# A new hand-written order for three engines at the start of an attention and experts kernel

## The chip, the cores and the metric

The program runs on one core of one Trainium2 chip. The metric is device time in microseconds for one execution; lower is better. TensorE (PE) multiplies, VectorE (DVE) and ScalarE (ACT) do elementwise work, GpSimd (POOL) scatters and gathers rows, and the sync engine (SP) issues the plain DMAs.

## The reference

Inputs are q, k, v and a complex decay a_re + i a_im, each 4 x 8 x 768 x 48 (batch, head, position, channel), and the weights of a layer of eight experts. The recurrence and the layer behind it:

```
mag = sqrt(a_re^2 + a_im^2);  a = (a_re + i a_im) * min(mag, 0.999) / (mag + 1e-6)
for t in 0..767:                       # per batch and head, S is 48 x 48, complex
    S = diag(a[t]) S + k[t] v[t]^T
    y[t] = q[t] Re(S)
x = y of all heads, 3072 rows x 384
logits = x @ w_gate + softplus(x @ w_noise) * noise
top 2 of 8 experts, weights = softmax of the two logits
out = sum over the two of weight * (relu(x @ w1[e]) @ w2[e])
```

## The kernel before

**Tiles.** Positions are cut into six groups of 128, and a tile is one group of one batch: 24 tiles n = 4 g + b. The decays are handled in pairs of tiles, m = 0 to 11, because two tiles fit one instruction of 768 columns. The first two pairs (`HALVES`) are handled in halves a and b of 384 columns.

**One tile's work** has short names, and the whole start is written with them: a letter for the engine (A ScalarE, D VectorE, P TensorE, G the gate on all three), a number for the step, and the pair or the tile.

- Pair: A1 takes the logarithm of a_re, A2 its negative exponential, D1 the tangent of the angle, D2 its square, A3 log(1 + tan^2), D3 the log of the squared magnitude, A4 and D4 the clamp; A5 is the arctangent (D5 adds the angle carried from the group before).
- Tile: P1 sums the angles along positions, D6 (A6 from the second group on) and D7 reduce them to a fraction of a turn; D8 takes the absolute value, A7 and A8 are cosine and sine (both by `Sin`). P2 sums the log magnitudes, A9 and A10 are exp of plus and minus that, and D9 scales q and k by them. D10 and D11 rotate q and k; P3 and P4 transpose them, A11 and A12 evict the transposes (qT, kT).
- P5a, P5b are the scores (four heads each), D12a, D12b mask them, P6 and D13 update the state, D14 to D16 decay it, P7a, P7b give the output, A13 evicts it, P8 turns it back and A14 writes the rows. G0 to G12 compute the gate of a group and the slots of its rows; then POOL scatters the rows to the experts' lists.

**The order.** `ORDER` lists some 700 such names. For each of the three engines the names that belong to it are chained (`order at the start`), so the engine issues them in exactly that order; engines run in order, and an instruction waits at the head of its engine until its operands and buffers are free. The place of a name in the list also sets where its function emits its code, loads included (`PLACE`, `pos`, `behind_key`). Work that isn't in the list is placed by step numbers (`P`) and a scheduler.

**Table runs.** `Ln` and `Exp` need one activation table, `Arctan` and `Sin` another. `phase(i, ...)` puts an activation into run i; a table load opens each run, every activation of the run comes behind it, and the next load behind all of them. The run's number is a formula of the tile: even for logarithms and exponentials, odd for arctangents and sines.

**Buffers that matter.** EE (the exponentials A9 and A10) has three buffers, and each is also read by a small store to DRAM, `es<-ee`, which SP issues. `cum` has two PSUM banks, shared by P1, P2, P8 and the gate; `ptr`, the transposes, has one. SP issues in its own order: the first pairs' decays, q and k and v, the gate's weights, eight transfers `xs<-none` that mark rows as empty, and only then `es<-ee`.

**The experts** follow: for each, x @ w1 and h @ w2 in a split of two fp32r parts (L649, L698), nearly all on TensorE.

Of the kernel before, what the change touches and what calls it, by code (L numbers as in the profile page):

```python
# [77 lines left out]
def kernel(  # L78
# [103 lines left out]
    for t in ecol:  # L182
# [20 lines left out]
        A12.1 D10.3 P1.4 A13.0 D5.3 P3.2 A6.4 D16.0 D7.4 P5a.1 A11.2 D13.2 P1.5 D4.3 P4.2 D12a.1 A6.5 D4.2 P1.6  # L203
        A12.2 D7.5 P7a.1 D11.3 A6.6 P1.7 A8.2 D8.2 P6.3 A6.7 D7.6 A7.2 D7.7 P2.4 D13.3 A8.3 P8.0 D8.3 P5b.1
        A14.0 A7.3 P3.3 D12b.1 A9.4 P5a.2 P7b.1 D12a.2 P5b.2 A10.4 A13.1 D9.4 P2.5 A11.3 D12b.2 P7a.2 A1.4 D10.4
        P8.1 A9.5 P7b.2 D11.4 A2.4 P4.3 A10.5 D1.4 P6.4 A13.2 A14.1 D9.5 P8.2 A12.3 P2.6 D2.4 A14.2 P3.4 A9.6
        D11.5 A3.4 P5a.3 D10.5 A10.6 A11.4 P2.7 D9.6 P5b.3 A1.5 D12a.3 D10.6 P4.4 A9.7 A2.5 D12b.3 P7a.3 A12.4
        D3.4 P7b.3 A10.7 D1.5 P3.5 A13.3 A4.4 D9.7 G0.0 A11.5 D2.5 P5a.4 G1.0 D10.7 P4.5 A3.5 D12a.4 P5b.4 A12.5
        D3.5 P8.3 D12b.4 P3.6 A4.5 D4.4 P5a.5 A14.3 A5.4 D14.0 D16.1 D15.0 G2.0 P5b.5 G3.0 D15.3 G4.0 D15.1
        P7a.4 D12b.5 A5.5 D5.4 P7b.4 D5.5 P1.8 A11.6 D13.4 P1.9 A6.8 D12a.5 A13.4 D7.8 P6.5 A6.9 D4.5 P1.10 D7.9  # L210
        P7a.5 D11.6 A6.10 A8.4 D8.4 P1.11 D11.7 A7.4 P4.6 D15.2 A6.11 P7b.5 D7.10 A12.6 D7.11 P8.4 D8.5 A8.5
        P5a.6 D13.5 A7.5 P6.6 D12a.6 A14.4 G5.0 P3.7 P5b.6 A11.7 G6a.0 G6b.0 P2.8 G6c.0 D12b.6 G7.0 A13.5 P4.7
        G8a.0 G8b.0 A9.8 G8c.0 G8d.0 A10.8 P7a.6 G8e.0 A12.7 G8f.0 G8g.0 D9.8 P2.9 G9.0 G8h.0 P7b.6 D11.8 A9.9
        A1.6 D10.8 P2.10 A13.6 D13.6 A2.6 P5a.7 G12a.0 G12b.0 A9.10 G12c.0 P3.8 D1.6 A10.9 A10.10 G10.0 D12a.7
        A11.8 P8.6 G12d.0 G11a.0 G12e.0 G12f.0 P5b.7 G11b.0 A14.6 G12g.0 D9.9 P4.8 D12b.7 P2.11 D9.10 A12.8
        P7a.7 D2.6 A1.7 P6.7 D10.9 A9.11 A3.6 P7b.7 D10.10 A2.7 D3.6 P3.9 A13.7 A10.11 D1.7 P5a.8 A11.9 D11.9
        G0.1 A4.6 D12a.8 P5b.8 G1.1 D2.7 P4.9 D13.7 A3.7 P8.7 D12b.8 A12.9 P6.8 D3.7 P8.5 A14.7 D11.10 A4.7
        P3.10 D14.1 D16.2 D15.6 A14.5 P5a.9 D15.4 A5.6 D15.5 G2.1 P7a.8 G3.1 D12a.9 G4.1 P5b.9 D15.7 A5.7 D5.6
        P7b.8 D5.7 P1.12 A11.10 D12b.9 P1.13 D4.7 A6.12 A13.8 P4.10 D7.12 A6.13 D9.11 P1.14 A12.10 D7.13 P7a.9
        D10.11 A6.14 A8.6 P8.8 D7.14 P7b.9 D8.6 A14.8 D4.6 A7.6 P1.15 D13.8 A13.9 P5a.10 A6.15 D7.15 P6.9  # L220
        D12a.10 A8.7 P5b.10 D8.7 D13.9 A7.7 P2.12 D11.11 G5.1 P8.9 D12b.10 P7a.10 A14.9 P3.11 G6a.1 G6b.1 G7.1
        G6c.1 A9.12 G8a.1 P7b.10 G8b.1 A10.12 G8c.1 G8d.1 A11.11 D9.12 P2.13 A13.10 G8f.1 D10.12 P4.11 G9.1
        A9.13 A1.8 G8e.1 P8.10 G12a.1 G8g.1 A10.13 P6.10 G12b.1 G8h.1 G12c.1 A14.10 D9.13 A12.11 G10.1 G12d.1
        P2.14 G11a.1 G12e.1 A2.8 G12f.1 G11b.1 G12g.1 D10.13 P5a.11 A9.14 D11.12 A10.14 P3.12 D9.14 P5b.11
        A11.12 D12a.11 P2.15 D10.14 P7a.11 A1.9 D12b.11 A9.15 P4.12 D13.10 A2.9 D1.8 P7b.11 A12.12 D1.9 P6.11
        A13.11 D2.8 A10.15 P3.13 D11.13 A3.8 P5a.12 D2.9 A11.13 G0.2 D3.8 A3.9 P4.13 D12a.12 G1.2 A4.8 G2.2
        D13.11 P5b.12 G3.2 A12.13 D3.9 P6.12 G4.2 D12b.12 A4.9 P5a.13 D14.2 D11.14 A5.8 P3.14 D12a.13 P5b.13
        D15.8 D4.9 P7a.12 A5.9 D12b.13 P8.11 D5.8 P7b.12 A14.11 D16.3 D15.9 P1.16 D5.9 A11.14 P1.17 D13.12 A6.16
        D15.10 A13.12 P4.14 D7.16 A6.17 D9.15 P7a.13 A12.14 D7.17 P1.18 D10.15 A8.8 P7b.13 D8.8 A6.18 D4.8 A7.8
        P3.15 D7.18 A13.13 P1.19 D15.11 A11.15 P8.12 A6.19 P6.13 A14.12 D7.19 P5a.14 D8.9 A8.9 D11.15 P2.16 A7.9  # L230
        D12a.14 P5b.14 G5.2 D13.13 P7a.14 D12b.14 A9.16 G6a.2 P6.14 G6b.2 G7.2 G6c.2 A10.16 G8a.2 G8b.2 D9.16
        P4.15 G8c.2 P7b.14 D11.16 A12.15 G8d.2 P2.17 A13.14 D13.14 G8f.2 D10.16 P5a.15 G9.2 A1.10 G12a.2 P2.18
        G8e.2 A9.17 A2.10 D12a.15 P3.16 G8g.2 G12b.2 A9.18 G8h.2 G12c.2 D1.10 P7a.15 A10.17 A11.16 G12d.2 D2.10
        G10.2 A10.18 P5b.15 G11a.2 A3.10 G12e.2 G12f.2 G11b.2 G12g.2 P2.19 D9.17 P4.16 D12b.15 A9.19 A1.11 D3.10
        P7b.15 A12.16 D10.17 P8.14 A2.11 D9.18 P6.15 A14.14 P3.17 D1.11 A10.19 A4.10 D11.17 P5a.16 A13.15 D2.11
        P8.13 A11.17 G0.3 D10.18 A3.11 P4.17 D12a.16 G1.3 A14.13 P5b.16 D3.11 A12.17 D13.15 P8.15 A4.11 D14.3
# [836 lines left out]
```

## Time and profile before

| | |
|---|---|
| median of 3 runs | 709.5 us (709.18 to 710.33) |
| profiled execution | 710.01 us, span 708.3 us |
| busy, VectorE | 411.2 us (58% of the span) |
| busy, ScalarE | 328.0 us (46%) |
| busy, GpSimd | 172.6 us (24%) |
| TensorE's share of the chain that ended last | 80% |

The span runs from the first to the last instruction of the profile; the execution's own time is 1.7 us longer. A share of busy time is a mean over stages: the attention part, with all four engines at work, takes roughly the first 250 us, the experts the rest. "Granted clock" is the share of TensorE's full clock (2.4 GHz) that was granted in a stretch; 0.50 is the lower of its two levels, 1.2 GHz.

### The profile page before, as it was taken

To read this page: it belongs to the slowest core of one execution; us is meant where nothing else is said; L and a number is where in the kernel's file an instruction comes from. 1 tells how busy PE (TensorE), PEld (TensorE's weight loads), DVE (VectorE), ACT (ScalarE), POOL (GpSimd) and SP (SyncE) were. 2 spreads that over 40 slices of the span, in tenths; PEclk is the share of its full clock that TensorE was granted. 3 is DMA by queue.
4 is the path that set the end of the run, shared out by engine and by line. 5 is a ranking of instruction groups with operands and counts; after the bars stand their busy time and mean duration, and the time that the engine had idled before them with its cause. 6 is when DMAs were issued, how large, how long until landed. Compare 5 with 4: busy or idle time off the path is not lost.

```text
span 708.3 us, 13293 instructions
## 1 busy us (share of the span) xinstructions
PE 666.2 (94%) x5120; PEld 590.7 (83%) x5120; DVE 411.2 (58%) x919; ACT 328.0 (46%) x553; POOL 172.6 (24%) x183
## 2 busy tenths in 40 slices
...
GB/s 315 255 217 211 268 181 127 174 200 131 94 92 277 178 72 249 130 84 187 59 80 264 30 91 169 129 90 169 132 40 175 179 37 178 173 23 68 65 33 36
...
## 3 DMA queue, kind: packets, MB, share of 16 engines
...
q0 software_dynamic: 9360, 27.54, 11.0%
...
## 4 chain that ended last, share of the span: by engine, by line
PE 80%; DVE 8%; ACT 5%; DMA 4%; issue 1%; SPq 1%; another core or an unknown queue 0%; POOL 0%; POOLq 0%; DVEq 0%; ACTq 0%
PE po L698 28%; PE ph L649 27%; PE ptr L354 4%; PE psc L363 4%; PE pY L412 2%; PE cum L307 2%; DMA raw<-in_moe_w_dram 2%; PE pY L414 2%; PE px L625 2%; PE pG L374 2%; PE po L704 2%; PE cum L331 1%; PE psc L649 1%; ACT t L248 1%; PE cum L427 1%
## 5 line engine op out<-in xcount | busy, mean ns | idle before, releaser
L698 PE MATMUL po<-w2h,h 128*128 128x384 f32 x768 | 203.9, 338 | 2.1 <-DVE ao L709 2.1
L649 PE MATMUL ph<-x,w1h 128*128 128x512 f32 (+2 forms) x720 | 187.2, 348 | 0.6 <-ACT x L630 0.5
L698 PEld LDWEIGHTS po<-w2h,h 128*128 128x128 f32 x768 | 139.4, 188 | 3.7 <-DVE ao L709 3.6
L649 PEld LDWEIGHTS ph<-x,w1h 128*128 128x128 f32 x720 | 125.7, 189 | 18.3 <-DVE h L655 1.3
L698 PE MATMUL po<-w2l,h 128*128 128x384 f32 x384 | 128.5, 335 | 0.0
L649 PE MATMUL ph<-x,w1l 128*128 128x512 f32 (+2 forms) x360 | 124.4, 347 | 0.0
L710 POOL DMA_INDIRECT out_dram<-ao,ox x52 | 50.9, 978 | 261.2 <-DVE ao L709 247.2
L497 POOL DMA_INDIRECT xs<-xr,sl x48 | 60.8, 1266 | 202.4 <-DVE qk L336 92.0
L655 DVE SCALAR_TENSOR_TENSOR h<-ph,h 128x512 fp32r<-128x512 f32 (+2 forms) x144 | 69.6, 505 | 67.5 <-ACT h L651 51.0
L651 ACT ACTIVATE h<-ph 128x512 fp32r<-128x512 f32 (+2 forms) x120 | 59.9, 507 | 102.0 <-PE ph L649 73.3
L709 DVE SCALAR_TENSOR_TENSOR ao<-po,gw,ao 128x384 f32<-128x384 f32 (+1 forms) x52 | 31.8, 614 | 125.1 <-PE po L698 124.8
L630 ACT CAST x<-px 128x512 fp32r<-128x512 f32 (+1 forms) x42 | 21.3, 518 | 125.5 <-PE px L625 125.5
L649 PEld LDWEIGHTS ph<-x,w1l 128*128 128x128 f32 x360 | 67.9, 189 | 7.9
L698 PEld LDWEIGHTS po<-w2l,h 128*128 128x128 f32 x384 | 72.2, 188 | 0.1
L674 POOL DMA_INDIRECT ao<-out_dram,ox x49 | 54.7, 1117 | 53.7 <-issue 31.7
L363 PE MATMUL psc<-qT,kT 112*128 112x128 f32 x384 | 54.1, 283 | 1.1 <-DVE h L655 0.6
L363 PEld LDWEIGHTS psc<-qT,kT 112*128 112x128 f32 x384 | 48.9, 196 | 5.9 <-issue 1.9
L586 ACT CAST w2h<-raw 128x768 fp32r<-128x768 f32 x32 | 26.5, 835 | 33.6 <-PE po L698 17.3
L414 PE MATMUL pY<-am,v 128*48 128x128 f32 x384 | 38.3, 275 | 1.6 <-DVE am L364 1.6
L587 DVE TENSOR_TENSOR w2l<-raw,w2h 128x768 fp32r<-128x768 f32 x32 | 30.4, 957 | 15.1 <-ACT w2h L586 14.2
L364 DVE TENSOR_TENSOR am<-psc,mask 128x512 f32<-128x512 f32 x48 | 32.8, 684 | 10.2 <-PE psc L363 8.6
L412 PE MATMUL pY<-qT,z 112*48 112x128 f32 x320 | 34.2, 279 | 0.2 <-DVE z L397 0.2
...
## 6 DMA issues: line engine op xcount, KB each, us to landing
...
```

The lines of the kernel that those rows point to most:

```text
L363: key(f"P5{'ab'[half]}.{n}", nc.tensor.matmul(p[:, j, :], KT[n][:, h, :], QT[n][:, h, :], start=True, stop=True))
L364: LAST['am'] = nc.vector.tensor_mul(AM[n][:, 4 * half:4 * half + 4, :], p, mask[:, None, :].to_broadcast([128, 4, 128]))
L412: x = nc.tensor.matmul(o, Z[b][:, h, :], QT[n][:, h, :], start=True, stop=False, skip_group_check=True)
L414: x = nc.tensor.matmul(o, V[n][:, h, :], AM[n][:, h, :], start=not g, stop=True, skip_group_check=True)
L497: d = nc.gpsimd.indirect_dma_start(out=xs, out_offset=bass.IndirectOffsetOnAxis(ap=sl[:, kk, b:b + 1], axis=0), in_=XR[g][:, lo + b, :], i ...
L649: LAST['m'] = nc.tensor.matmul(p[:, :c], W1[e, kk][i][:, f * 128:(f + 1) * 128], XW[w, kk][:, j, 0:c], start=(m == 0), stop=(m == len(ms) ...
L651: nc.scalar.activation(h[:, 0:c], p[:, :c], AF.Relu)
L655: LAST['h'] = nc.vector.scalar_tensor_tensor(h[:, dst:dst + b - a], p[:, a:b], 0.0, h[:, a:b].bitcast(F32), op0=OP.max, op1=OP.subtract)
L674: nc.gpsimd.indirect_dma_start(out=ao[j][0:w, :], out_offset=None, in_=out, in_offset=bass.IndirectOffsetOnAxis(ap=OX[e][0:w, j:j + 1], ax ...
L698: LAST['po'] = key(f"PO.{e}.{j}", nc.tensor.matmul(p[:, :DM], HT[w, f][i][:, o:o + 128], W2[f // 2][k2][:, f % 2, :], start=(m == 0), stop ...
L709: nc.vector.scalar_tensor_tensor(a, p[0:n, :DM], g, a, op0=OP.mult, op1=OP.add)
L710: d = nc.gpsimd.indirect_dma_start(out=out, out_offset=bass.IndirectOffsetOnAxis(ap=OX[e][0:n, j:j + 1], axis=0), in_=a, in_offset=None, b ...
```

## The change

Four edits. `ORDER` is a new list, of 717 names instead of 710; it ends a little further on (P5a.17, P5b.17, P7a.17, A5.11, A13.16, D4.10, D5.10, D5.11 and D9.19 are in it, D10.18, D13.15, P3.18 and P6.16 no longer; D15.13 in place of D15.15). `phase` takes a name: the run's number is found by walking the list and raising it each time the kind of table changes; activations behind the list keep the formula, shifted by the difference at the list's end. The first pair's decays are loaded whole instead of in halves. The tiles of `softplus` have two buffers. The functions' other lines only pass the name.

```diff
     ORDER = """
-        A1a.0 A2a.0 D1a.0 A1b.0 D2a.0 A2b.0 A3a.0 D1b.0 D3a.0 D2b.0 A4a.0 A3b.0 D4a.0 A1a.1 D3b.0 P2.0 A2a.1
-        A1b.1 D1a.1 A4b.0 D2a.1 A2b.1 D4b.0 A3a.1 D1b.1 P2.1 A9.0 D3a.1 A10.0 D2b.1 A4a.1 D9.0 A3b.1 A9.1 D3b.1
-        A10.1 D4a.1 A4b.1 D9.1 A5a.0 D4b.1 A5b.1 P1.0 A5a.1 A5b.0 P1.1 D6.0 D7.0 P1.2 D6.1 D7.1 D8.0 A8.0 P1.3
-        D6.2 A7.0 D7.2 D6.3 P2.2 D10.0 D7.3 P3.0 D10.1 A8.1 P2.3 D8.1 A11.0 D11.0 A7.1 D11.1 P6.0 A1.2 P4.0
-        D13.0 P6.1 A9.2 D13.1 A2.2 A1.3 D1.2 A9.3 D2.2 A2.3 A12.0 D1.3 A3.2 P3.1 D2.3 A10.2 D3.2 A3.3 P5a.0 D9.2
-        A10.3 A11.1 D3.3 A4.2 P4.1 D10.2 A4.3 D11.2 P5b.0 A5.2 D12a.0 P6.2 D9.3 P7a.0 D12b.0 A5.3 D5.2 P7b.0
...
+        A1a.0 A1b.0 A2a.0 A2b.0 D1a.0 D1b.0 D2a.0 A1a.1 D2b.0 A3a.0 A2a.1 D3a.0 A1b.1 D1a.1 A4a.0 D2a.1 A2b.1
+        D4a.0 A5a.1 D1b.1 P2.0 D2b.1 A5a.0 A5b.1 P1.0 A5b.0 A9.0 D6.0 D7.0 A3b.1 A10.0 D3b.1 A3b.0 P1.1 D9.0
+        A4b.1 A3a.1 D3b.0 P1.2 D6.1 A4b.0 D3a.1 D7.1 A4a.1 D6.2 P1.3 A8.0 D8.0 D7.2 D6.3 D4a.1 A7.0 D7.3 D4b.0
+        A8.1 D8.1 P2.1 D11.0 A7.1 P2.2 D10.0 A9.1 P6.0 D4b.1 P3.0 D13.0 A10.1 A1.2 D9.1 P2.3 A11.0 D11.1 A1.3
+        P4.0 D10.1 A2.2 P6.1 A12.0 D1.2 A9.2 D13.1 P3.1 A2.3 D2.2 P5a.0 A10.2 D1.3 A9.3 A11.1 P5b.0 D12a.0 A3.2
+        D2.3 P4.1 A10.3 D12b.0 P7a.0 A3.3 D3.2 P7b.0 A12.1 D3.3 A4.2 P5a.1 D9.2 A4.3 P5b.1 D4.2 A13.0 D11.2 A5.2
+        P8.0 D10.2 P6.2 D12a.1 P3.2 A14.0 D5.2 A5.3 P7a.1 D13.2 P1.4 A11.2 D5.3 P1.5 A6.4 D9.3 P4.2 A6.5 D7.4
...
-    def phase(i, *args, **kw):
+    def usual(k):
+        a, i = k.split(".")
+        a, i = a.rstrip("ab"), int(i)
+        if a[0] == "G":
+            return 2 * min(i + 3, NG)
+        if a in ("A9", "A10"):
+            return 2 * (i // B) + 2 if i > 1 else 0
+        return 2 * (2 * i // B) + (a in ("A5", "A7", "A8"))
+    RUN, run, last = {}, 0, None
+    for k in ORDER:
+        if k.split(".")[0].rstrip("ab") in ("A1", "A2", "A3", "A4", "A5", "A7", "A8", "A9", "A10", "G5", "G7", "G9"):
+            run += (usual(k) - run) % 2
+            RUN[k], last = run, k
+    shift = run - usual(last)
+    def phase(name, *args, **kw):
+        i = RUN.get(name, usual(name) + shift)
         if i not in phases:
...
-        for j in range(2) if m == 0 else (slice(0, 2),):
-            nc.sync.dma_start(RE[m][:, j], a_in[m, 0][:, j])
-            nc.sync.dma_start(IM[m][:, j], a_in[m, 1][:, j])
+        nc.sync.dma_start(RE[m], a_in[m, 0])
+        nc.sync.dma_start(IM[m], a_in[m, 1])
...
-    c, w, u = (pool.tile(shape, F32, name=tag + x) for x in "cwu")
+    c, w, u = (pool.tile(shape, F32, name=tag + x, bufs=2) for x in "cwu")
```

Later in the new list, the names that the prediction speaks of stand so:

```
... P7b.1 A9.4 D12a.2 P5b.2 D13.3 P2.5 D12b.2 A13.1 A10.4 P7a.2 ...
... D3.4 A12.4 P7b.3 D10.6 A13.3 P3.5 ...
... G0.1 D15.4 A12.9 D11.10 P7a.8 G1.1 D4.7 A5.6 G2.1 ...
... G3.2 D15.11 A12.13 D5.8 P6.12 A13.12 G4.2 ... A6.17 G8e.1 P1.18 ... G12g.1 ...
... P2.12 D12b.10 G6a.1 P7b.9 A9.12 ... P2.13 G8b.1 A13.9 D13.9 D9.12 A11.11 P7a.10 ...
... G8g.2 G12b.2 G8h.2 G12c.2 D10.16 A9.17 G10.2 ...
```

## Rows read from the trace of the kernel before

**Rows 1.** the page, first part: busy us (share of the span), instructions

```profile
PE 666.2 (94%) x5120; PEld 590.7 (83%) x5120; DVE 411.2 (58%) x919; ACT 328.0 (46%) x553; POOL 172.6 (24%) x183
```

**Rows 2.** windows: us, busy us of each engine (instructions), TensorE clock, DMA share, GB/s

```profile
0.00:34.86 34.86, 13.52 (x96) 6.63 (x96) 24.79 (x61) 24.65 (x46) 5.41 (x27) 0.98 0.86 289
20.00:30.00 10.00, 7.13 (x88) 4.34 (x88) 8.42 (x14) 7.17 (x9) 0.00 (x0) 1.00 1.01 322
34.86:43.21 8.35, 8.20 (x80) 7.82 (x80) 8.31 (x13) 8.33 (x11) 0.00 (x0) 0.66 0.65 150
43.21:160.00 116.79, 116.17 (x1389) 94.53 (x1390) 107.96 (x222) 102.21 (x162) 24.73 (x18) 1.00 0.65 199
160.00:300.00 140.00, 130.86 (x1298) 111.73 (x1297) 105.47 (x339) 77.60 (x141) 39.81 (x40) 1.00 0.47 154
```

**Rows 3.** TensorE's waits: whole span, then 43-190 us (first, last of six)

```profile
PE ptr L354 <- ACT kT L355: 5.4, 1, 5.4
...
PE pY L414 <- DVE am L364: 0.8, 2, 0.5
...
PE cum L307 <- DVE t L302: 0.2, 1, 0.2
```

**Rows 4.** TensorE's timeline: start us, us, line, operation, tiles [idle before <-releaser]

```profile
34.86 1.96 PE L354 MATMUL ptr<-ident,qh 128*112 128x128 f32 x8 [5.38 <-ACT kT L355]
36.61 1.92 PE L363 MATMUL psc<-qT,kT 112*128 112x128 f32 x8
38.32 1.91 PE L354 MATMUL ptr<-ident,kh 128*112 128x128 f32 x8
40.03 1.30 PE L363 MATMUL psc<-qT,kT 112*128 112x128 f32 x8
41.26 0.93 PE L374 MATMUL pG<-v,kh 128*48 128x48 f32 x32
...
43.21 0.91 PE L307 MATMUL cum<-t,tri_t 128*128 128x384 f32 x2 [0.15 <-DVE t L302]
```

**Rows 5.** chain that ended last: start us, us to the next piece, what

```profile
52.81 0.88 PE ptr L354 x8
53.69 0.89 PE psc L363 x8
54.58 0.57 PE pY L414 x8
...
57.47 0.59 PE cum L427 x4
```

**Rows 6.** ScalarE's timeline

```profile
3.31 0.52 ACT L248 ACTIVATE t<-re 128x384 f32<-128x384 f32 x1 [1.20 <-DMA re<-in_a_dram]
...
5.53 0.52 ACT L248 ACTIVATE t<-re 128x384 f32<-128x384 f32 x1 [1.06 <-DMA re<-in_a_dram]
...
16.30 1.76 ACT L248 ACTIVATE t<-t 128x384 f32<-128x384 f32 x4
...
26.13 0.93 ACT L248 ACTIVATE tr<-tf,b_cos 128x768 f32<-128x768 f32 x1
27.07 1.28 ACT L247 ACT_TABLE_LOAD   x1
28.37 0.84 ACT L248 ACTIVATE t<-re 128x768 f32<-128x768 f32 x1
...
32.58 0.49 ACT L248 ACTIVATE ee<-cum 128x384 f32<-128x384 f32 x1 [1.44 <-DMA es<-ee]
```

**Rows 7.** SP's DMA issues

```profile
12.08 0.33 SPq L259 DMA_DIRECT2D im<-in_a_dram  x1
...
22.09 6.94 SPq L783 DMA_DIRECT2D xs<-none  x8
29.14 1.87 SPq L338 DMA_DIRECT2D es<-ee  x2
```

**Rows 8.** ScalarE by shape, 0-160 us: busy us, mean ns | idle before

```profile
L355 ACT ACTIVATE kT<-ptr 112x1024 f32<-112x1024 f32 x15 | 15.4, 1024 | 2.0 <-PE ptr L354 2.0
```

More of the change, by code (lines that the diff above doesn't have):

```diff
@@ L202 @@
-        A10.3 A11.1 D3.3 A4.2 P4.1 D10.2 A4.3 D11.2 P5b.0 A5.2 D12a.0 P6.2 D9.3 P7a.0 D12b.0 A5.3 D5.2 P7b.0
[L203 to L236, printed above, removed]
@@ new lines @@
+        P4.0 D10.1 A2.2 P6.1 A12.0 D1.2 A9.2 D13.1 P3.1 A2.3 D2.2 P5a.0 A10.2 D1.3 A9.3 A11.1 P5b.0 D12a.0 A3.2
+        D2.3 P4.1 A10.3 D12b.0 P7a.0 A3.3 D3.2 P7b.0 A12.1 D3.3 A4.2 P5a.1 D9.2 A4.3 P5b.1 D4.2 A13.0 D11.2 A5.2
+        P8.0 D10.2 P6.2 D12a.1 P3.2 A14.0 D5.2 A5.3 P7a.1 D13.2 P1.4 A11.2 D5.3 P1.5 A6.4 D9.3 P4.2 A6.5 D7.4
+        D7.5 P1.6 A12.2 D11.3 P1.7 A8.2 D10.3 P6.3 A6.6 D8.2 A6.7 D7.6 P3.3 A7.2 D7.7 D16.0 P2.4 D8.3 A8.3
+        D12b.1 P5a.2 A7.3 D4.3 P7b.1 A9.4 D12a.2 P5b.2 D13.3 P2.5 D12b.2 A13.1 A10.4 P7a.2 A11.3 D9.4 P8.1 P7b.2
@@ new lines @@
+        A9.5 D11.4 A14.1 P4.3 A10.5 D10.4 A13.2 P6.4 A1.4 D9.5 P8.2 A12.3 P2.6 D10.5 A2.4 P3.4 D11.5 A14.2 P5a.3
+        D1.4 A11.4 P5b.3 D2.4 A9.6 A10.6 P2.7 D12a.3 A3.4 D12b.3 P4.4 A9.7 D9.6 A1.5 P7a.3 D3.4 A12.4 P7b.3
+        D10.6 A13.3 P3.5 A2.5 D11.6 G0.0 A11.5 D1.5 P5a.4 A4.4 D2.5 P4.5 G1.0 A10.7 D4.4 P5b.4 A3.5 D12a.4 A12.5
+        G2.0 P8.3 D3.5 A14.3 P3.6 D12b.4 A4.5 G3.0 D14.0 P5a.5 G4.0 D15.0 A5.4 D4.5 P7a.4 D12a.5 P5b.5 D15.2
+        A5.5 D5.4 P7b.4 D5.5 P1.8 A11.6 D13.4 P1.9 D15.3 A6.8 D15.1 A13.4 P4.6 D7.8 A6.9 D12b.5 P1.10 A12.6 D7.9
@@ new lines @@
+        P7a.5 D9.7 A6.10 A8.4 D8.4 P1.11 D10.7 A7.4 P7b.5 D7.10 A6.11 D16.1 P3.7 A13.5 D7.11 D8.5 A8.5 P2.8 A7.5
+        P8.4 P5a.6 A14.4 G5.0 P6.5 D12a.6 P5b.6 D13.5 A9.8 G6a.0 A11.7 D11.7 P6.6 A10.8 D12b.6 P7a.6 G7.0 G6b.0
+        D9.8 P2.9 G6c.0 D10.8 P7b.6 A1.6 G8a.0 D11.8 A9.9 P4.7 A13.6 G8b.0 D13.6 A10.9 P2.10 G8c.0 A12.7 G8d.0
+        D9.9 P8.6 A9.10 P6.7 G8f.0 A14.6 D10.9 A10.10 P5a.7 G9.0 D11.9 A2.6 P3.8 D12a.7 P2.11 G8e.0 A11.8 D9.10
+        P5b.7 A9.11 D1.6 A1.7 P7a.7 D12b.7 A10.11 A2.7 P4.8 D2.6 P7b.7 D1.7 A12.8 P8.5 D10.10 A13.7 P3.9 A3.6
@@ new lines @@
+        D2.7 P5a.8 A14.5 A11.9 D3.6 P8.7 D13.7 P5b.8 A3.7 D12a.8 A14.7 P4.9 D3.7 A4.6 P6.8 D12b.8 A4.7 D14.1
+        D16.2 G0.1 D15.4 A12.9 D11.10 P7a.8 G1.1 D4.7 A5.6 G2.1 P7b.8 G3.1 D15.5 G4.1 D9.11 P3.10 A13.8 D5.6
+        P5a.9 A5.7 D13.8 A11.10 P8.8 D5.7 P1.12 A14.8 D10.11 P5b.9 A6.12 G12a.0 D7.12 P1.13 G12b.0 D12b.9 P4.10
+        A6.13 G12c.0 D12a.9 P1.14 D7.13 A12.10 G8g.0 D4.6 P7a.9 A6.14 G12d.0 A8.6 G8h.0 P1.15 D7.14 G12e.0 D8.6
+        G10.0 A6.15 D15.7 P3.11 A7.6 G11a.0 D7.15 G12f.0 G11b.0 P5a.10 A8.7 G12g.0 D8.7 D15.6 A7.7 P6.9 D12a.10
```

48 lines of the change are left out of this document (31 added, 17 removed).

## The prediction, made before the changed kernel was run

> **What bounds the kernel now.** I read four views, in this order. The page's first part: TensorE is busy for 666.2 us of the 708.3 us span [rows 1]. So there are 42 us without TensorE work, and a change that removes no matmul can win only from those, and from matmuls that run at the lower clock. Second, the windows show where they are: up to 34.86 us TensorE is busy for 13.5 us, that is 21.3 us idle; from 43.21 to 160 us it idles for 0.6 us, from 160 to 300 us for 9.1 us [rows 2]. Third, TensorE's waits: the one big entry that is not the first load is 5.4 us for ScalarE's kT, the eviction A12.0 [rows 3]. Fourth, the timelines of that place. TensorE starts P3.1 at 34.86 after 5.38 us of idling; the clock has fallen meanwhile, and P3.1, P5a.0, P4.1 and P5b.0 are followed by the next group after 1.75, 1.71, 1.71 and 1.23 us [rows 4], where such groups step 0.88 and 0.89 us later [rows 5]. A12.0 was late because ScalarE, in order, stood 1.44 us before A9.3 at 32.58, until the store es<-ee had landed, and because it had reached that run of its list only at 28.37, after the table load at 27.07 [rows 6].
>
> From 34.86 us on TensorE works nearly back to back. The sum is therefore a ledger of matmul work: how much more of it the new order has behind it at a given time.
>
> **The change, part by part.** (1) *Table loads.* In the old rule a run's number follows from the tile; in the new rule it rises whenever the order passes from an exponential or logarithm to an arctangent or sine, or back. Counted along both lists, the old one has loads 0 to 12, the new one 0 to 14: the start is cut into logs, four arctangents, logs, four sines. So two loads are added, both before 21 us. A switch is measured at 27.07: the sine before it ends at 26.13 + 0.93 = 27.06, the next activation starts at 28.37, so 1.31 us [rows 6]; two cost 2.6 us of ScalarE's time.
>
> The Trainium skill (ScalarE: Activation LUTs, What ACT_TABLE_LOAD costs) gives 1283 ns for the load and about 1380 ns more for a drain, 2.66 us for each switch to another set, and its rule is to batch activations by set. The trace has the first figure (1.28 us) and not the drain. By the Trainium skill's figure the two loads would cost 5.3 us instead of 2.6 us, and the lead worked out below would by an estimate be 1.6 us smaller, since 1.1 us of the 2.7 us would fall into a wait.
>
> (2) *The first load whole.* The first pair's logarithms were in halves before too; what changes is that both halves now come with one DMA of 384 KB. A1a.0 started at 3.31 with half the bytes, A1b.0 waited until 5.53 for its half [rows 6]. Both now start between these ends; I take 4.0. It decides nothing: the fifth activation, A1a.1, needs the second pair's data, the third 384 KB in the queue, which I put at 7.0 us; with 3.5 or 4.5 in place of 4.0 everything behind 7.1 us stays, and up to 1.1 us of lateness there falls into the wait for A9.3 (below).
>
> (3) *softplus with two buffers.* In the new list G8e.1 (which reads the tile) stands behind G4.2 (which writes it), so the second buffer lets the list be followed. It costs memory and no time.
>
> (4) *The order up to tile 16.* I laid the start out instruction by instruction: each engine in list order, each instruction when its operands, its PSUM bank and its engine are ready, durations from rows. The old list laid out in the same way gives A9.3 at 32.6, P3.1 at 34.9 and P1.4 at 43.3 us; the rows have 32.58, 34.86 and 43.21 [rows 4, 6]. The new list, by ScalarE:
> - Logs of run 0: A1a.0 4.0; A1a.1 7.1, A3a.0, A2a.1, A1b.1, A4a.0, A2b.1 at 0.41 to 0.53 us a step, end 9.9.
> - Load to 11.3. Four arctangents, 1.76 us for four [rows 6], end 13.0. Load to 14.3.
> - Run 2, eight half activations of which A4b.1, A4b.0 and A4a.1 each wait for a 0.55 us step of VectorE: end 19.0. Load to 20.3.
> - Four sines, 0.76 to 0.83 us a step (0.93 us for one [rows 6]), end 23.5. Load to 24.9. The old list was there at 28.37, so ScalarE leads by 3.5 us though it has loaded twice more.
> - A9.1, A10.1, A1.2, A11.0, A1.3, A2.2, A12.0 (29.0 to 30.0), A9.2, A2.3, A10.2, end 31.5. A12.0 now stands before A9.3, so P3.1 starts at 30.1, P5a.0 at 31.0, P5b.0 at 31.9.
> - A9.3 needs the first of three buffers, which es<-ee reads. That store stands in SP's queue behind the eight xs<-none transfers, issued from 22.09 to 29.03, and was issued at 29.14 [rows 7]; nothing in the change moves it ahead of them. So A9.3 again at 32.6, 1.1 us after ScalarE is ready. A11.1 (1.02 us for one eviction [rows 8]) ends at 34.0: P4.1 34.1, P7a.0 and P7b.0 until 36.1. A12.1 ends at 36.8: P5a.1 36.9, P5b.1 37.8. A4.3 ends at 38.3, load to 39.7, A13.0 until 40.3: P8.0 40.4, P6.2, P3.2, P7a.1 and then P1.4 at 43.1 us.
>
> P1.4 starts when it did (43.21), but five units more lie behind it: P5a.1 and P5b.1 (0.89 each), P3.2 (0.88), P7a.1 (0.57), P8.0 (at most 0.59, 0.5 taken) [rows 5]: 3.7 us, and 0.1 us for the earlier start: 3.8 us. Of that 2.8 us are the four groups that no longer run at the low clock (6.40 us from 34.86 to 41.26 [rows 4] against 3.54); the rest is idle time that is filled.
>
> What is late next: laid out further, the new list makes TensorE wait for A13.1 (P7a.2, 0.6 us), A12.4 (P3.5, 0.8), G1.1 (G2.1, 1.2), A13.9 (P7a.10, 0.4) and G8h.2 (G10.2, 0.6): 3.6 us up to 176 us. The old list's own waits from 43 to 190 us are six kinds, 0.8 us down to 0.2 us, together 2.5 us [rows 3]. That takes back 1.1 us. VectorE and ScalarE don't fall behind: at 176 us they lead by 4 and 3 us. The second gate's late half (G8e.1 to G12g.1) moves from 132 to 152 us, so POOL's scatters of that group come later; their reader, the buffer of tile 16's rows, isn't wanted before 185 us.
>
> (5) *Where the lead could grow.* SP waits before issuing the fourth pair's imaginary part until D1b.1 has ended, 12.08 us [rows 7]; in the new list D1b.1 ends at 10.7, so SP can be 1.4 us ahead with all that it issues behind. Whether es lands sooner depends on whether the transfers or SP set the pace up to 29 us: ends 0 and 1.1 us (then ScalarE is the bound), and 0.3 us taken, nearer to the transfers, since the 16 DMA engines are busy throughout from 20 to 30 us (share 1.01 [rows 2]).
>
> Sum: 3.8 - 1.1 + 0.3 = 3.0 us. After the list TensorE has 520 us of dense work whose amount is the same, so the lead should arrive at the end. The profiled execution took 710.01 us (span 708.3 and 1.7 around it), 0.5 us over the median: 707.0 us on that footing, 706.5 us as median.
>
> **Rivals.** *A: given back behind the list.* From 160 to 300 us TensorE idles for 9.1 us [rows 2], in stretches that no list governs, where gate, last tiles and first expert interleave. If work there falls differently, most of the 3.0 us can go. For it: these idles are three times the lead. Against: the lead is on all three engines, and the new list carries more of ScalarE's and VectorE's work (D4.10, D5.10, D5.11, D9.19, A13.16). 708.2 to 709.8 us.
>
> *B: more than the ledger.* es lands at 31.5 and the idles behind 160 us shrink because VectorE leads by 4 us and TensorE's waits there are partly for VectorE. 4 to 5.5 us: 704.0 to 705.5 us.
>
> *C: slower, by the clock.* The new start has matmuls in small groups: laid out, 10.6 us of work in the 16 us from 24.4 to 40.4. If the clock falls there and stays low, every us of dense work costs another (1.75 against 0.88 us for P3 [rows 4, 5]). The lead is gone once 3 us of matmul work more than laid out run at 1.2 GHz, and it is slower by over 1.4 us from 4.4 us on; with 7 us it is 4 us slower, 713.5 us. For it: the clock did fall in this stretch of the old order, to a mean of 0.66 between 34.86 and 43.21 [rows 2]. Against: that came after 5.4 us without a matmul; from 20 to 30 us, with 7.13 us busy of 10, the clock was granted in full [rows 2], and the new gaps from there on are 0.7 to 1.8 us.
>
> The Trainium skill (TensorE: Matmul & The Clock Gate, Part 1) says that half rate is the default and activity lifts it; the trace agrees so far as it fell behind the longest gap, 5.4 us.
>
> *D: it doesn't do what it says.* If es lands late (34 us) or the loads are placed ahead of evictions, the new front gains only 1.5 us: 708.0 us, inside A's and the forecast's bounds.
>
> **Chances.** The likeliest, the lead kept (2 to 4 us, 705.5 to 707.5 us), 0.60; A with D 0.20; B 0.10; C 0.10. A measurement can tell 0.2%, 1.4 us, from no change. Faster than 708.1 us: the forecast, B and a little of D, 0.71; within: 0.17; slower than 710.9 us: C and the worst of A, 0.12. The range that holds 8 in 10 runs from 704.3 us (half of B left out) to 709.8 us (all of A in, C out).
>
> **What would show it.** Fifteen table loads, two more before 21 us; the first sine near 20 us and the load behind the sines near 23.5 us. A9.3 again waiting for es<-ee, ending near 32 us. P3.1 near 30 us, no gap over 3 us between 24 and 43 us, and the granted clock at full after 22 us. P1.4 near 43 us with P5a.1, P5b.1, P8.0, P3.2 and P7a.1 before it. P7b.15 some 3 us earlier than before. I am wrong if A9.3 doesn't wait for the store, if the clock in 24 to 43 us is below full, or if the lead at 176 us is there and the end isn't earlier.

## The result: 1.3% slower, and the profile after

The changed kernel took 719.0 us (median of 4, 718.2 to 719.2) beside 709.4 us for the kernel before on the same chip: ratio 1.013 [1.011, 1.015], 9.6 us slower. The prediction said 706.5 us. The profiled execution took 718.8 us with a span of 717.0 us.

The page's first part after the change; against [rows 1] TensorE's busy time is 3.6 us more, and the span 8.7 us more:

```profile
PE 669.8 (93%) x5120; PEld 592.2 (83%) x5120; DVE 411.8 (57%) x919; ACT 331.2 (46%) x555; POOL 168.2 (23%) x183
```

The same windows of the changed kernel, to be laid beside [rows 2]:

```profile
0.00:34.86 34.86, 19.27 (x120) 11.31 (x120) 24.99 (x63) 28.27 (x50) 5.46 (x27) 1.00 0.84 290
20.00:30.00 10.00, 7.39 (x51) 4.71 (x51) 7.82 (x13) 7.97 (x11) 0.00 (x0) 1.00 1.02 321
34.86:43.21 8.35, 7.25 (x93) 5.96 (x92) 8.35 (x12) 8.32 (x12) 0.00 (x0) 1.00 0.88 193
43.21:160.00 116.79, 112.31 (x1356) 91.16 (x1355) 109.43 (x225) 101.88 (x160) 12.72 (x12) 1.00 0.61 181
160.00:300.00 140.00, 124.67 (x1257) 106.53 (x1256) 101.03 (x329) 74.29 (x136) 46.28 (x46) 0.98 0.49 159
```

Up to 43 us the change does what was forecast. Before 34.86 us 24 matmuls more have run (120 against 96 [rows 2]): P3.1, P5a.0 and P5b.0, 2.7 us of work by the steps of [rows 5]. TensorE is busy 5.75 us longer there; the other 3.1 us are a lower clock up to 28 us (see the steps that held). From 34.86 to 43.21 us the clock is at full where it had been 0.66. From 43.21 to 160 us TensorE idles for 4.5 us instead of 0.6 us, and from 160 to 300 us for 15.3 us instead of 9.1 us. TensorE's timeline of the front:

```profile
32.01 1.09 PE L367 MATMUL ptr<-ident,qh 128*112 128x128 f32 x8 [0.47 <-ACT kT L368]
32.94 1.95 PE L376 MATMUL psc<-qT,kT 112*128 112x128 f32 x16
34.98 1.06 PE L367 MATMUL ptr<-ident,kh 128*112 128x128 f32 x8
...
37.65 2.05 PE L376 MATMUL psc<-qT,kT 112*128 112x128 f32 x16 [0.60 <-ACT kT L368]
...
43.24 1.24 PE L321 MATMUL cum<-t,tri_t 128*128 128x384 f32 x3
```

P1.4 (43.24) starts where it did, with P5a.1 and P5b.1 (37.65) done, as laid out; the idle of 5.38 us before P3.1 [rows 4] is 0.47 us. So the lead was there, and it was lost later. The largest loss, in the timeline of all engines:

```profile
158.38 0.99 POOL L510 DMA_INDIRECT xs<-xr,sl  x1 [16.64 <-DVE am L377]
...
164.28 0.17 PE L490 MATMUL cum<-ohs,ones_b 128*128 128x8 bf16 x1
...
164.86 0.17 PE L490 MATMUL cum<-ohs,ones_b 128*128 128x8 bf16 x1 [0.41 <-issue]
165.57 0.18 PE L492 MATMUL cum<-ohs,tri_b 128*128 128x8 bf16 x1 [0.54 <-issue]
...
166.99 0.19 PE L490 MATMUL cum<-ohs,ones_b 128*128 128x8 bf16 x2 [1.24 <-issue]
167.61 0.98 POOL L510 DMA_INDIRECT xs<-xr,sl  x1 [0.30 <-issue]
...
169.84 0.27 PE L490 MATMUL cum<-ohs,ones_b 128*128 128x8 bf16 x4 [1.21 <-issue]
169.90 0.85 ACT L264 ACTIVATE t<-re 128x768 f32<-128x768 f32 x1 [6.37 <-PE cum L492]
...
170.23 0.19 DVE L494 TENSOR_TENSOR pos<-cum,base_run 128x32 f32<-128x32 f32 x1 [5.05 <-PE cum L490]
```

G10.2, fourteen matmuls of 8 columns of which only the first has to wait for an operand, is spread over 5.7 us: TensorE starts an instruction every 0.7 us or so, and "issue" says that it waits for no semaphore that the profile shows. ScalarE (6.37 us) and VectorE (5.05 us) wait behind it. All of this stands beside POOL's scatters, eight in one train from 158.38 to 168.6 us. In the kernel before, the same eight stand in two trains of four, from 137.1 and from 152.7 us, because the gate's late half was done by 132 us.

The hole has a second part. Behind it the granted clock falls to 0.50, the lower level, for 6.8 us:

```profile
168.03:174.85 6.82, 5.22 (x52) 4.38 (x52) 3.94 (x12) 4.25 (x8) 3.10 (x5) 0.50 0.51 173
```

TensorE is busy for 5.22 us of this at half speed, so about 2.6 us of the loss is the clock's (an estimate; eight transposes take 1.94 us at 169.96 and 1.04 us at 175.17 us).

### The profile page after: what moved, and what is told of

It is laid out like the page before. It is cut to its first block, busy times and chain, and to the rows that moved or that the text cites. A ratio compares the mean times of both kernels' runs of the same rounds, so it can differ in the third digit from the quotient of the medians.

```text
span 717.0 us, 13304 instructions
## 1 busy us (share of the span) xinstructions
PE 669.8 (93%) x5120; PEld 592.2 (83%) x5120; DVE 411.8 (57%) x919; ACT 331.2 (46%) x555; POOL 168.2 (23%) x183
## 3 DMA queue, kind: packets, MB, share of 16 engines
q0 software_dynamic: 9360, 27.54, 11.0%
## 4 chain that ended last, share of the span: by engine, by line
PE 77%; DVE 10%; ACT 5%; DMA 4%; issue 3%; another core or an unknown queue 0%; SPq 0%; POOL 0%; POOLq 0%; DVEq 0%; ACTq 0%
PE po L711 28%; PE ph L662 27%; PE ptr L367 4%; PE psc L376 3%; PE pY L425 2%; PE px L638 2%; PE pY L427 2%; PE pG L387 1%; DMA v<-in_v_dram 1%; PE cum L321 1%; PE psc L662 1%; PE po L717 1%; DVE qk L349 1%; DVE kh L357 1%; DVE am L377 1%
## 5 line engine op out<-in xcount | busy, mean ns | idle before, releaser
L510 POOL DMA_INDIRECT xs<-xr,sl x48 | 55.6, 1158 | 212.1 <-DVE z L410 113.4
L376 PE MATMUL psc<-qT,kT 112*128 112x128 f32 x384 | 51.7, 279 | 0.9 <-ACT kT L368 0.9
L376 PEld LDWEIGHTS psc<-qT,kT 112*128 112x128 f32 x384 | 47.0, 191 | 5.3 <-issue 1.9
L377 DVE TENSOR_TENSOR am<-psc,mask 128x512 f32<-128x512 f32 x48 | 32.5, 684 | 11.4 <-PE psc L376 8.2
```

The source lines that it names most:

```text
L376: key(f"P5{'ab'[half]}.{n}", nc.tensor.matmul(p[:, j, :], KT[n][:, h, :], QT[n][:, h, :], start=True, stop=True))
L377: LAST['am'] = nc.vector.tensor_mul(AM[n][:, 4 * half:4 * half + 4, :], p, mask[:, None, :].to_broadcast([128, 4, 128]))
L510: d = nc.gpsimd.indirect_dma_start(out=xs, out_offset=bass.IndirectOffsetOnAxis(ap=sl[:, kk, b:b + 1], axis=0), in_=XR[g][:, lo + b, :], i ...
```

## The experiments

Eighteen runs, of fourteen kernels, were made on five chips. The chips fall into two kinds by what the kernel before takes on them: 709.1, 708.5 and 709.6 us on three of them (as in the result above), 703.4 and 703.1 us on two. This difference turned out to be part of the answer. Times are medians; the ratio is to the kernel before on the same chip.

### First chip: the kernel before takes 703.4 us

The four expectations here were written for a chip of 709 us, so their ranges can be neither met nor missed; what counts is the difference to the kernel before.

**e1_gates_early.** In the new list, G8e to G12g of groups 0 and 1 moved back to where they stood relative to the other work.

```diff
-... G8d.1 P7b.10 ... A6.17 G8e.1 P1.18 ... G12g.1 D11.15 ...
+... G8d.1 G8e.1 P7b.10 ... P8.10 G12a.1 G8g.1 ... G11b.1 G12g.1 A9.14 ...
```

> The changed kernel with the late halves of the first two gates (G8e to G12g of groups 0 and 1) put back to where they stood relative to the other work in the old list; everything else as changed, so the two waits on PACE spread the scatters again. Theory T (the loss comes from POOL's scatters standing back to back in trains of 6 and 8, during which TensorE and ScalarE get their instructions late): trains of 2 to 4 as before, no 6 us hole at 163 to 170 us, 706 to 709 us, so 10 to 13 us under the changed kernel. Rival O (the new list's own waits and its instruction mix from 97 to 170 us lose the lead, the trains only coincide): 715 to 719 us. Rival F (a rest of 3 us lost in the trains of group 2 and later, which this doesn't move): 709 to 712 us.

700.9 us, 0.9973 [0.9949, 0.9996].

**e2_pace_only.** The new list untouched; the scatters of groups 0 to 2 wait for later tiles.

```diff
-(0, 1): 8, (0, 2): 9, (0, 3): 10, (1, 1): 11, (1, 2): 12, (1, 3): 13, (2, 1): 15, (2, 2): 15, (2, 3): 16,
+(0, 1): 9, (0, 2): 10, (0, 3): 11, (1, 1): 14, (1, 2): 14, (1, 3): 15, (2, 1): 16, (2, 2): 16, (2, 3): 17,
```

> The changed kernel, list untouched; only the tiles whose xT the scatters of groups 0 to 2 wait for are raised, so that from 155 us on the scatters come as 2, 4, 4, 4, 2 and not as 8, 2, 4, 2. Theory T: the hole at 163 to 170 us goes or shrinks to under 2 us, and the time falls by 4 to 8 us, to 711 to 715 us; what stays is what trains of 4 cost. Rival O: G10.2 and A1.10 stand where they stood, the hole stays, 717 to 720 us. If the late scatters hold up the first expert's rows instead, the time stays too, but with a wait on xg after 195 us.

702.4 us, 0.9981 [0.9962, 1.0000].

**e3_old_with_train.** The kernel before, with the eight scatters of group 1 in one train.

```diff
-(1, 1): 11, (1, 2): 12, (1, 3): 13,
+(1, 0): 13, (1, 1): 13, (1, 2): 13, (1, 3): 13,
```

> The kernel before, with one line changed: all eight scatters of group 1 wait for tile 13's xT, so they come back to back near 157 us as in the changed kernel; list, loads and buffers as before. Theory T: TensorE's instructions are issued 0.5 to 1.3 us apart near the end of the train, a hole of 4 to 7 us, 713 to 717 us. Rival O: no hole, 709 to 711 us, since the old list is the one that runs.

702.6 us, 0.9987 [0.9969, 1.0005]: no price, though the train is there. My theory of that hour (trains cost, everywhere) missed.

**e5_old_list.** The changed code with the old list.

> The changed code (free table runs, first load whole, softplus with two buffers) with the old list in place of the new one: 13 table loads again. Theory T and rival O alike put the whole loss into the list: 708.5 to 710.5 us. If the whole first load or the second softplus buffer had a price of their own, 711 us or more.

702.8 us, 0.9997 [0.9980, 1.0013]. Free table runs, the whole first load and the second softplus buffer have no price of their own.

### Second chip: 709.1 us

> The changed kernel itself, unaltered, as a control. The first four experiments ran on a chip where the kernel before takes 703.4 us and where no engine of any kernel shows a gap that ends in issue or remote between 43 and 260 us, the old list with all eight scatters in one train included; in the traces from which the prediction was judged, the kernel before took 709.4 us and has such gaps at the ends of trains. Theory T (scatter trains alone): 710 us or more here too, with the hole at 163 to 170 us. Theory T2 (a train stalls the engines only on a chip or in a condition in which it also delays them in the kernel before, by some us): where the kernel before runs at 703 us, this one runs at 700 to 702 us, with the 3 us of the forecast and no hole; where it runs at 709 us, 717 to 720 us. Rival O (the list's own waits): 9 us above the kernel before on any chip.

c1_after is the changed kernel itself: 718.6 us, 1.0144 [1.0124, 1.0165].

> Again the changed kernel with the late halves of the first two gates put back early, now beside the changed kernel on one chip. Theory T2: on a chip where the kernel before takes 703 us, within 1 us of the changed kernel; where it takes 709 us, 8 to 12 us under the changed kernel. Theory T: 8 to 12 us under it on any chip. Rival O: within 3 us of the changed kernel on any chip.

c2 is e1 again: 713.0 us, 1.0064 [1.0044, 1.0084], 5.6 us under the changed kernel beside it. That was less than the 8 to 12 us expected, and it is still 3.9 us over the kernel before, though its trains are of two and four again.

> Again the kernel before with the eight scatters of group 1 in one train behind tile 13. Theory T2: no price where the kernel before takes 703 us (702 to 704 us), 4 to 7 us where it takes 709 us, with TensorE's instructions issued far apart at the end of the train. Rival O: no price on any chip.

c3 is e3 again: 718.0 us, 1.0125 [1.0108, 1.0142], 8.9 us more where 4 to 7 us were expected. One line of PACE makes the old list as slow as the new one, here and not there. Twelve microseconds from the first scatter of the train; the columns are those of [rows 2]. First on the chip of 703.4 us, then on this one:

```profile
156.65:168.65 12.00, 11.79 (x161) 9.70 (x159) 10.80 (x36) 9.74 (x20) 8.72 (x8) 1.00 0.65 205
```

```profile
158.64:170.64 12.00, 5.20 (x69) 4.33 (x68) 3.66 (x6) 4.71 (x8) 8.05 (x8) 0.78 0.55 186
```

The program is the same, POOL does the same eight instructions, and in the second the other engines do less than half as much. In the timeline VectorE and ScalarE stand idle, and "remote" says that this view names nobody who holds them:

```profile
164.47 0.96 DVE L344 TENSOR_TENSOR kh<-qk,tr 128x768 f32<-128x768 f32 x1 [3.93 <-remote]
...
168.75 0.69 DVE L364 TENSOR_TENSOR am<-psc,mask 128x512 f32<-128x512 f32 x1 [3.33 <-remote]
...
169.46 0.49 ACT L248 ACTIVATE ee<-cum 128x384 f32<-128x384 f32 x1 [6.33 <-remote]
...
169.50 0.67 PE L414 MATMUL pY<-am,v 128*48 128x128 f32 x4 [6.80 <-DVE am L364]
```

The trace's semaphore records name it. The first three wait for the semaphore that only TensorE's instructions raise, and they start 0.02 to 0.03 us behind its records at 164.44, 168.73 and 169.44 us. The matmuls that raise it have their recorded (modelled) ends at 159.72, 160.81 and 161.45 us, so TensorE's signals came 4.7 to 8.0 us behind them; in e3 they come 0.01 to 0.03 us behind. So here too it is TensorE that holds the others, by late signals and not by late starts in its records.

### Third chip: 708.5 us

**x_full, x_thin, x_drop.** The old list, and eight scatters more in one train, into a tensor that nobody reads; in x_thin rows of 16 elements, in x_drop a bound of 0. So that the group's own scatters are done before, two entries of its pace are moved too, and six of these now stand in one train (136.8 to 147.8 us in x_full).

```diff
+xe = nc.dram_tensor("xe", [E * N, ROW], F32, kind="Internal").ap()      # x_thin: [E * N, 16]
...
-(1, 2): 12, (1, 3): 13,
+(1, 2): 'A12.13', (1, 3): 12,
...
+d = nc.gpsimd.indirect_dma_start(out=xe, out_offset=..., in_=none, in_offset=None,
+                                 bounds_check=E * N - 1, oob_is_err=False)   # x_drop: bounds_check=0
+behind.append((d, 13))
```

> The old list with all its own scatters in time (those of group 1 before 155 us), and eight more scatters of a constant tile, 128 rows of 1600 bytes each, into a tensor that nobody reads, in one train behind tile 13's xT. Theory T2 and all its forms: on a chip where the kernel before takes 709 us 6 to 10 us more, with VectorE, ScalarE and TensorE each starting instructions late between 160 and 171 us; where it takes 703 us, within 1 us. Rival: the hole came from the late rows of group 1 themselves (somebody waits for them), then no price here.

720.4 us, 1.0160 [1.0128, 1.0193], 11.9 us more, over the range. The train of six has a part in it: laid against the kernel before, the eviction A13.n of x_full ends 2.0 us later behind that train and 10.0 us later behind the train of eight.

> As x_full, but the eight added scatters write rows of 64 bytes instead of 1600. Form B of the theory (the bytes, that is the packets on the DMA engines, hold up the others): the price falls to under 2 us. Form N (the number of scatter instructions or of their rows and descriptors): the price stays, 6 to 10 us on a chip where the kernel before takes 709 us.

720.2 us, 1.0161 [1.0144, 1.0178], 11.7 us more.

> As x_full, but the bound of the added scatters is 0, so that practically every row is dropped and nothing is written. Form B: no price. Form N with the written rows as the cause: no price. Form P (POOL's own work on the descriptors, or what it does while it prepares them, is what holds up the others): the price stays, 6 to 10 us on a chip where the kernel before takes 709 us.

719.9 us, 1.0157 [1.0141, 1.0174], 11.4 us more. Nobody waits for these rows, and it doesn't matter how many bytes are written. In the twelve microseconds from the train's start, x_full moves 185 GB/s, x_thin and x_drop 51, and TensorE works 7.08, 7.06 and 6.74 us:

```profile
161.91:173.91 12.00, 7.08 (x84) 4.64 (x82) 6.10 (x23) 3.50 (x7) 8.49 (x8) 0.92 0.55 185
```

```profile
161.91:173.91 12.00, 7.06 (x84) 4.73 (x82) 6.17 (x23) 3.57 (x7) 8.43 (x8) 0.94 0.17 51
```

```profile
162.25:174.25 12.00, 6.74 (x91) 5.16 (x87) 5.86 (x14) 4.77 (x9) 8.29 (x8) 0.85 0.20 51
```

So it is not the bytes. Packets are there in all three: POOL's queue has 9872 of them in x_full and in x_drop and 9616 in x_thin, beside 9360 in the kernel before. What the three share is POOL's eight instructions; that it is POOL's own work in them, and not what they put into the queue, is not shown. In x_drop another group of matmuls than G10.2 is caught, pG<-v,kh, with the same spacing of 0.7 us or twice that:

```profile
170.16 0.20 PE L375 MATMUL pG<-v,kh 128*48 128x48 f32 x1 [0.41 <-issue]
170.90 0.37 PE L375 MATMUL pG<-v,kh 128*48 128x48 f32 x2 [0.54 <-issue]
172.31 0.33 PE L375 MATMUL pG<-v,kh 128*48 128x48 f32 x2 [1.04 <-issue]
173.03 0.24 PE L375 MATMUL pG<-v,kh 128*48 128x48 f32 x1 [0.38 <-issue]
```

**f1_pairs.** e1's list, and PACE names instructions of ScalarE instead of tiles, so that the scatters of groups 0 to 4 come in pairs.

```diff
-(1, 1): 11, (1, 2): 12, (1, 3): 13, (2, 1): 15, (2, 2): 15, (2, 3): 16, ...
+(1, 1): 'A13.11', (1, 2): 'A13.12', (1, 3): 'A13.13', (2, 1): 'A13.15', (2, 2): 'A13.16', (2, 3): 'A11.18', ...
```

> The changed kernel with the gates' late halves early (as in the experiments e1 and c2) and the scatters of groups 0 to 4 released two at a time, each pair behind an instruction of ScalarE some 5 us after the pair before, so that no train is longer than two up to 255 us. Theory T2 (trains delay the other engines on a chip where the kernel before takes 709 us; a train of four costs some 2.5 us there, one of two next to nothing): 699 to 703 us on any chip, faster than the kernel before on both kinds. Rival O2 (what c2 lost against e1, 8 to 12 us, is not the trains of four but a slower memory or queue of that chip): 708 to 713 us there. If the first expert's rows then come too late, a wait of TensorE on xga near 206 us.

708.3 us, 0.9988 [0.9965, 1.0011]: over the 699 to 703 us expected, at the edge of the rival's 708 to 713 us.

### Fourth chip: 703.1 us

> The kernel before with POOL's 48 scatters replaced by plain stores of the same rows from SP's queue, to fixed places of xs instead of the computed ones (that is what its output lacks); list, gate, loads and all other work as before. Theory T2 (what POOL does in its scatter instructions slows the starts of instructions on the other engines, on most chips): on a chip where the kernel before takes 709 us, 700 to 703 us, and no gap that ends in issue or remote before 260 us. If the chip's slowness is something else: 707 us or more.

714.1 us, 1.0149 [1.0124, 1.0173]: a miss. TensorE lost 5.5 us between 43 and 160 us to waits for VectorE's z (5.0 us in two waits), without a single "issue" gap; stores added to SP's queue have a price of their own, and the pair can't measure the lead.

> The changed kernel with the same replacement. Theory T2 with the forecast's lead (3 us, kept behind the list): 2 to 4 us under d_before. Theory T2 with rival A of the prediction (lead given back behind 160 us, where no list governs): within 1.2 us of d_before. Rival O (the new list's own waits make the loss): 8 us or more above d_before.

703.6 us, 0.9993 [0.9979, 1.0007], 10.5 us under d_before and outside all that was expected; inconclusive for the same reason.

> The changed kernel, its list untouched, with the scatters of groups 0 to 4 released two at a time, each pair behind an instruction of ScalarE some 5 us after the pair before (so group 1's eight scatters take from 155 to 177 us and not 10 us). Theory T2: no hole at 163 to 170 us; on a chip where the kernel before takes 709 us, 706 to 711 us, that is 8 to 12 us under the changed kernel, as f1 was. Rival O: 717 to 720 us there. Where the kernel before takes 703 us: 701 to 703 us.

703.2 us, 1.0001 [0.9988, 1.0015]. As expected for this kind of chip, and so no test of the price.

> The kernel before with only the scatters of groups 2 to 4 released in pairs some 5 us apart (their trains of four at 172, 208, 218 and 233 us are gone). Theory T2, with 1 to 2.5 us for each train of four: 703 to 706 us on a chip where the kernel before takes 709 us. If it is the number of scatters and not their trains: 708 to 710 us.

703.8 us, 0.9999 [0.9985, 1.0013]; likewise.

### Fifth chip: 709.6 us

> The changed kernel once more, unaltered, beside the kernel before on one chip. Theory T2: where the kernel before takes 709 us, 717 to 720 us; where it takes 703 us, no hole, no gap that ends in issue before 260 us, and 700 to 703 us: the lead of the forecast is there at 195 us and is partly given back between 195 and 216 us by waits for kT, ee and xga, as in e2 and f2. Rival O: 9 us above the kernel before on any chip.

718.9 us, 1.0122 [1.0095, 1.0149]. This chip is of the slower kind again, and the time is within the 717 to 720 us expected.

**s1_singles.** f1 with the second scatter of each pair behind an instruction of its own; the pace (not shown) now names one for nearly every scatter.

```diff
-n_y = PACE.get((g, lo + b))
+n_y = PACE.get((g, lo + b, kk) if kk else (g, lo + b))
```

> The changed kernel with the gates' late halves early and the scatters of groups 0 to 4 released one at a time, each behind an instruction of ScalarE 2 to 5 us after the one before. Theory T2, if the delay builds up while POOL goes from scatter to scatter without a pause: 700 to 704 us where the kernel before takes 709 us (f1, with pairs, took 708.3 us there), and 700 to 702 us where it takes 703 us. If every scatter has its price, whatever stands around it: as f1, 706 to 709 us where the kernel before takes 709 us.

704.6 us, 0.9927 [0.9901, 0.9952]: 5.1 us under the kernel before and 14.3 us under the changed one; 0.6 us over the 700 to 704 us expected. So it is not the number of scatters, which is 48 in the changed kernel, f1 and this one alike, but how close they stand. Its scatters around the old hole, and a train of four that is left (another, of three, stands at 145.0 us):

```profile
158.47 0.97 POOL L516 DMA_INDIRECT xs<-xr,sl  x1 [6.52 <-ACT ga4w L265]
162.53 0.97 POOL L516 DMA_INDIRECT xs<-xr,sl  x1 [3.08 <-ACT ee L265]
...
168.00 1.01 POOL L516 DMA_INDIRECT xs<-xr,sl  x1 [1.54 <-DVE qh L358]
169.64 0.97 POOL L516 DMA_INDIRECT xs<-xr,sl  x1 [0.63 <-ACT ee L265]
172.51 3.36 POOL L516 DMA_INDIRECT xs<-xr,sl  x1 [1.90 <-ACT kT L369]
176.17 0.97 POOL L516 DMA_INDIRECT xs<-xr,sl  x1 [0.30 <-ACT t L265]
177.45 0.97 POOL L516 DMA_INDIRECT xs<-xr,sl  x1 [0.30 <-ACT kT L369]
178.73 1.10 POOL L516 DMA_INDIRECT xs<-xr,sl  x1 [0.30 <-issue]
```

Of TensorE's waits from 43 to 190 us the longest stands right behind that train, at 180.03 us:

```profile
PE cum L460 <- issue: 2.0, 1, 2.0
```

It starts 0.05 us behind the end of what it reads, ScalarE's lt, and lt had waited for TensorE's signal:

```profile
179.71 0.27 ACT L454 COPY lt<-cum 128x128 f32<-128x128 f32 x1 [2.51 <-remote]
```

> f1 again, beside the two others. Theory T2: where the kernel before takes 709 us, 707 to 709 us as in f1; where it takes 703 us, 700 to 702 us as e1.

706.7 us, 0.9964 [0.9942, 0.9985], between the kernel before and the singles, 0.3 us under the 707 to 709 us expected.

## Why the prediction was wrong, step by step

**The step that failed** is in part (4): "The second gate's late half (G8e.1 to G12g.1) moves from 132 to 152 us, so POOL's scatters of that group come later; their reader, the buffer of tile 16's rows, isn't wanted before 185 us." I asked only who reads the scattered rows, and put the move at nothing. PACE spreads the scatters only while the tiles that it names lie ahead. In the changed kernel the gate's late half was done at about 157.6 us and the first scatter went at 158.4 us; the tiles that the later ones wait for, 11, 12 and 13, were evicted by 138.2, 147.2 and 160.6 us, each before its scatters' turn, and so eight went off in one train. On this kind of chip such a train costs about 9 us by itself: c3, with the old list, lost 8.9 us. Nothing in the old list has a train of eight before 258 us, so its trace could not price one. But it had a hint: an idle of VectorE of 1.18 us, marked "remote", at the end of a train of four (244.23 us).

How the loss adds up can be read by laying the changed kernel's trace against e2's, which has the same list and differs in PACE and chip; likewise before against e5. By how many us the eviction A13.n (xT<-pY) ends later, and the span:

```
n                   8    10    13    14    15    16    18    19    23   span
changed - e2       1.1   3.4   3.4   9.9  10.3  13.2  13.2  13.7  15.2  16.3
before - e5        0.6   1.0   1.7   2.0   2.3   2.3   2.3   4.7   7.4   7.2
```

The changed kernel loses 2.3 us at its first train (eight scatters from 119.6 to 133.9 us, one pause of 1.6 us), 6.5 us at the train of eight (most of the clock's part in them), 2.9 us at the train of four from 183.5 us; 1.1 us were there before the first train, and 3.5 us come in smaller pieces. The old list loses 1.7 us in small pieces up to A13.15, and 2.4 us between A13.18 and A13.19, where a train of four stands. From 160 to 300 us TensorE idles for 4.1 us in e5 and for 9.1 us in [rows 2], so 5.0 us of what rival A took for a matter of the order come with the kind of chip. The two spans on this kind of chip differ by 16.3 - 7.2 - 0.4 = 8.7 us, where 0.4 us is what e2 is shorter than e5.

**Steps that held.** (1) Fifteen loads, two more, at 1.28 us each; the sines start at 20.12 us (laid out 20.3). (2) A1a.0 at 3.94 us (4.0 taken), A1a.1 at 7.15 us (7.1). (3) and the rest of the code: no price (e5). (4) up to 43 us: P1.4 at 43.24 us (laid out 43.1). P3.1 came 1.9 us late, at 32.01 us; that did not reach P1.4. ScalarE's rows of the front:

```profile
3.94 0.94 ACT L264 ACTIVATE t<-re 128x384 f32<-128x384 f32 x2 [1.83 <-DMA re<-in_a_dram]
...
7.15 0.52 ACT L264 ACTIVATE t<-re 128x384 f32<-128x384 f32 x1 [1.26 <-DMA re<-in_a_dram]
...
20.12 0.84 ACT L264 ACTIVATE tr<-tf 128x768 f32<-128x768 f32 x1
...
23.78 1.28 ACT L263 ACT_TABLE_LOAD   x1
...
33.05 0.88 ACT L264 ACTIVATE ee<-cum 128x384 f32<-128x384 f32 x2
```

Rival C did come for a while, without a lasting price. TensorE up to 31 us:

```profile
22.37 2.92 PE L345 MATMUL cum<-t,tri_l 128*128 128x384 f32 x4 [2.05 <-DVE t L305]
25.23 1.52 PE L387 MATMUL pG<-v,kh 128*48 128x48 f32 x32
26.68 1.75 PE L367 MATMUL ptr<-ident,qh 128*112 128x128 f32 x8
28.27 0.81 PE L345 MATMUL cum<-t,tri_l 128*128 128x384 f32 x2
...
30.62 0.93 PE L387 MATMUL pG<-v,kh 128*48 128x48 f32 x32
```

Up to 28 us it steps at about half of the later rate, as at the lower level: four matmuls of 384 columns in 2.92 us, then two in 0.81 us; P6.0 in 1.52 us, P6.1 in 0.93 us; P3.0 in 1.75 us, P3.1 in 1.09 us. That is 2.5 us more than at the later rate, and it lies on the way to P3.1, because A11.0 waits for P3.0 (1.79 us). The windows' 1.00 does not show it: the trace's first clock record starts at 28.08 us (20.06 us in the kernel before), and this view counts a stretch without one as full. A clock below full in 24 to 43 us was a named sign of being wrong.

A9.3 is the second of the two at 33.05 and waits for no store, which I had named as a sign of being wrong; es<-ee was issued at 27.94 instead of 29.14 us (step 5), and ScalarE came to A9.3 too late to wait for it.

**Rival A** came true on a chip where trains cost nothing. On the chip of 703.4 us the first exponentials of tiles 20 to 23 start at 196.57 us with the old list (e5) and 193.72 us with the new one (e2), a lead of 2.9 us; at the end 0.4 us of it is left (spans 701.1 and 700.7 us). First e5, then e2:

```profile
196.57 0.85 ACT L264 ACTIVATE ee<-cum 128x384 f32<-128x384 f32 x2
```

```profile
193.72 0.85 ACT L264 ACTIVATE ee<-cum 128x384 f32<-128x384 f32 x2
```

TensorE's waits in e2 from 190 to 222 us say where it went, behind the list:

```profile
PE ptr L638 <- DMA xga<-xs: 1.4, 1, 1.4
PE ptr L367 <- ACT kT L368: 1.0, 2, 0.9
PE cum L345 <- ACT ee L264: 0.9, 1, 0.9
```

The wait for xga belongs to e2's later scatters. In e1, which has them early, it is absent, and 2.5 us of the forecast's 3.0 us arrive (700.9 against 703.4 us; the interval runs from 0.3 to 3.6 us). So the ledger was sound as far as this can tell, and another order keeps the lead; the price of the trains was outside it.

**Left open.** The changed kernel itself never ran on a chip of the faster kind; that it would take some 701 to 703 us there is argued from e1, e2 and f2, not shown. The singles ran only on the slower kind. Why c2 stays 3.9 us over the kernel before no run shows. By what way POOL's scatter instructions make TensorE late, and why only on some chips, no run here shows either. One rival is untested, the recording itself, since all times here are of recorded executions. On the slower kind each trace has 138 to 176 instructions of TensorE, VectorE and ScalarE whose semaphore record is missing or more than 0.15 us behind their end, on the faster kind 6 at most; and all but two at most of them in each trace end during an indirect DMA of POOL or within 1 us behind one. Whether these chips would pay the price without the recording is open.
